# Second MLP layer by seven products of half-size blocks instead of eight, in a fused attention and MLP kernel

## The chip, the cores and the metric

The kernel runs on one core of one Trainium2 chip. The metric is device time in microseconds; the time before is the median of three runs, 341.34 us (341.12 to 341.46). Five engines work beside each other, each with its own queue in program order: TensorE (PE in the profile; its weight loads are listed apart as PEld), VectorE (DVE), ScalarE (ACT), GpSimd (POOL) and SyncE (SP), which here issues DMAs alone.

## The reference

Attention with a decay, then a two-layer MLP with gelu on its output, seen as 4608 tokens of 512 values; w_in is 512 by 2048, w_out 2048 by 512:

```python
batch, n_heads, seq, head_dim = (8, 8, 576, 64)
scores = scale * np.matmul(q, k.transpose(0, 1, 3, 2))
log_f = np.log(np.clip(f, 0.0001, 1.0))
cum = np.cumsum(log_f, axis=-1)
decay = cum[:, :, :, None] - cum[:, :, None, :]
scores = np.where(causal, -1000000000.0, scores + decay)
scores = scores - np.max(scores, axis=-1, keepdims=True)
attn = np.exp(scores)
attn = attn / (np.sum(attn, axis=-1, keepdims=True) + 1e-09)
return np.matmul(attn, v).astype(np.float32)
...
x = np.ascontiguousarray(attn_out.transpose(0, 2, 1, 3)).reshape(B * S, H * D)
...
h = x @ w_in
g = 0.5 * h * (1.0 + np.tanh(c * (h + 0.044715 * h * h * h)))
return (g @ w_out).astype(np.float32)
```

## The kernel before

**Attention** goes by quads: 16 groups of four heads of one batch, two quads to a batch. For a quad, `scores` (L202) makes the products of keys and queries in three rounds of row-tiled matmuls (32 rows, one head each) into PSUM pool `psS` (two buffers of two banks), and ScalarE takes the exponential into `pt` (L228). GpSimd masks the diagonals (`mask`, L234) and multiplies values by their decay weights (`make_vw`, L178); in FRONT some of both is on VectorE. `denominators` (word D in the tables) and `attn_out` (word V, twice a quad) are column-tiled products of 32 columns a head (L288) into pool `psO`, which has one buffer; for D, VectorE follows with a transpose, a reciprocal and a transpose (L307 to L311), for V with one multiplication into `xT` (L319). The next D or V needs psO free of these.

**The MLP** goes by chunks of 512 tokens, 0 to 8. `mlp_in` (L322) makes two blocks of 128 hidden units (a "pr") with eight matmuls of 128x512 into a psS tile; ScalarE's gelu writes them to `gT` (L337). `gT` has two buffers, by the chunk's parity. Chunk 0 goes through `mlp_in_half` (L339), in halves of 256 tokens. `mlp_out` (L357) makes the second layer: for each 128 tokens it accumulates 16 matmuls of 128x512 (stationary `gT`, moving `w_out_sb`) in a bank of pool `psM` (L91, two buffers), and VectorE copies the bank to `o_st` (L373), from where SP's queue stores it (L375).

**Order.** It is written by hand. `mlp_out` is a generator: `out_part(c, n)` (L446) pulls its next n matmuls, so that pieces of the second layer fill TensorE's time while attention waits for ScalarE. With `tiled`, which the words f of the tables and all of `beside` (L505) use, each pulled step is four column-tiled matmuls of 32 columns instead of one of 128. Setup, chunk 0, attention quads 0 to 6 and most of chunk 1 follow the word table FRONT: S and H are scores, D and V as above, M and m masks on GpSimd and VectorE, I is `mlp_in` of one pr, F and f are `out_part`, LK, LQ and LV loads, TK and TQ transposes on VectorE, X loads the table of the exponential. From chunk 2 the main loop (L550 to L564) alternates: the rest of chunk c-1's second layer, the first layer of chunk c, and in its midst `prepare` (transposes of the next quads' keys and queries on VectorE), then `pair` (L524), which runs quads 2c+3 and 2c+2 in five stages of scores, D or V and a piece of chunk c's second layer. From chunk 7 on there is no attention left: first and second layers follow each other.

Of the kernel before, what the change touches and what calls it, by code (L numbers as in the profile page):

```python
# [8 lines left out]
FP32 = mybir.dt.float32  # L9
BF16 = mybir.dt.bfloat16  # L10
AF = mybir.ActivationFunctionType
# [5 lines left out]
def kernel(  # L17
# [10 lines left out]
    nc = tc.nc  # L28

    B, H, S, D = q.shape  # L30
# [7 lines left out]
    D_MODEL, D_FF = moe_w_in.shape  # L38
    N_DT = D_MODEL // 128
    N_FT = D_FF // 128  # L40
# [4 lines left out]
    NP = D_FF // 256  # L45
    CH = 512
    NCH = B * S // CH
# [11 lines left out]
    QA = 256  # L59
# [17 lines left out]
        V.0.1.1 V.0.0.1 WO.0 J.0.1 D.1.1 J.0.0 WO.1@LV.1.1 V.1.1.1 V.1.0.1 J.0.3 WO.2@WI.1 VW.3 J.1.0 WO.3 LK.3 LQ.3 J.1.1 TQ.2 J.1.3 LQ.4  # L77
        LX.1.0@WO.2 TK.2 J.0.2 J.1.2 X LK.4 F.0.6 TK.3 B.3.256 S.2.0 LK.5 F.0.9 S.2.2 F.0.10 S.2.1 TQ.3 TQ.4 F.0.10 LV.2.0@LK.5 m.2.1 vw.2
        TK.4 S.3.0 f.0.1 M.2.2 CL.2 LQ.5 M.2.0 D.2 f.0.6 S.3.1 m.3.0 F.0.6 V.2.0 S.3.2 TK.5 LK.6 M.3.2 f.0.7 V.2.1 CL.3
        S.4.1 m.3.1 LQ.6 F.0.6 TQ.5 H.4.2.1 D.3 H.4.0.1 LQ.7 VW.4 H.4.0.0 V.3.1 v.3.0 f.0.3 H.4.2.0 CL.4 I.1.0 m.4.1 LV.2.1@LQ.5 I.1.5  # L80
        TQ.6 m.4.2.3 I.1.1 I.1.7 LV.3.0@LQ.7 m.4.2.2 TK.6 M.4.0 I.1.3 I.1.2 I.1.4 I.1.6 X F.1.8 S.5.0 F.1.2 F.1.14 S.5.1 D.4 M.5.0 f.1.9
        S.5.2 V.4.0 m.5.2.3 f.1.6 VW.5 V.4.1 CL.5 m.5.2.2 LQ.8 S.6.0 f.1.6 M.5.1 D.5 f.1.4 S.6.1 V.5.1 f.1.7 V.5.0 vw.6 S.6.2
        m.6.1 M.6.2.2 m.6.0 m.6.2.3 LK.7 LK.8 CL.6 LX.3.1@LK.6
    """

    singles = ctx.enter_context(tc.tile_pool(name="singles", bufs=1))
    ostage_pool = ctx.enter_context(tc.tile_pool(name="ostage", bufs=3))
    den_pool = ctx.enter_context(tc.tile_pool(name="den", bufs=2))
# [20 lines left out]
    gT = many(2, [128, N_FT, CH], BF16, "gT")  # L109
# [205 lines left out]
    def attn_out(i, x, spare=False, part=None):  # L315
        b, u = i // QPB, i % QPB
        po = product(i, [(32 * h, lambda t, h=h: vw[i % 2][:, t, h, x:D:2], h) for h in range(4)], spare, part)
        s0, s1 = (0, S) if part is None else parts[part]
        nc.vector.tensor_mul(xT[:, 2 * u + x, S * b + s0:S * b + s1], po, rbs[i, part])  # L319


    def mlp_in(c, prs):  # L322

        tiles = [psS.tile([128, 2, 512], FP32, name="ps_h", tag="s") for _ in prs]
        for pr, ph in zip(prs, tiles):
            for dts in (range(N_DT - 1), range(N_DT - 1, N_DT)):
                for j in range(2):
                    ft = 2 * pr + j
                    for dt in dts:
                        nc.tensor.matmul(  # L330
                            ph[:, j, :],
                            w_in_sb[:, dt, 128 * ft:128 * ft + 128],
                            xT[:, dt, CH * c:CH * (c + 1)],
                            start=(dt == 0), stop=(dt == N_DT - 1),
                        )
        for pr, ph in zip(prs, tiles):
            nc.scalar.activation(gT[c % 2][:, 2 * pr:2 * pr + 2, :], ph, AF.Gelu_apprx_tanh)  # L337

    def mlp_in_half(half, g):  # L339

        ph = psS.tile([128, 2, 512], FP32, name="ps_h", tag="s")
        n0 = QA * half
        for dts in (range(N_DT - 1), range(N_DT - 1, N_DT)):
            for j in range(4):
                ft = 4 * g + j
                for dt in dts:
                    nc.tensor.matmul(  # L347
                        ph[:, j // 2, QA * (j % 2):QA * (j % 2) + QA],
                        w_in_sb[:, dt, 128 * ft:128 * ft + 128],
                        xT[:, dt, n0:n0 + QA],  # L350
                        start=(dt == 0 and j % 2 == 0), stop=(dt == N_DT - 1),
                        skip_group_check=True,
                    )
        nc.scalar.activation(gT[0][:, 4 * g:4 * g + 4, n0:n0 + QA],
                             ph.rearrange("p a (b n) -> p (a b) n", n=QA), AF.Gelu_apprx_tanh)

    def mlp_out(c):  # L357

        for n in range(CH // 128):
            r0 = CH * c + 128 * n  # L360
            last = c == NCH - 1 and n == CH // 128 - 1
            st = ostage_pool.tile([128, D_MODEL], FP32, name="o_st", tag="o")
            for (m0, m1) in ((0, 384), (384, 512)) if last else ((0, D_MODEL),):
                pso = psM.tile([128, D_MODEL], FP32, name="pso", tag="m")
                for ft in range(N_FT):
                    cols = 32 if by_columns else 128
                    for c0 in range(0, 128, cols):
                        nc.tensor.matmul(pso[c0:c0 + cols, m0:m1],  # L368
                                         gT[c % 2][:, ft, 128 * n + c0:128 * n + c0 + cols],
                                         w_out_sb[:, ft, m0:m1],  # L370
                                         start=(ft == 0), stop=(ft == N_FT - 1), skip_group_check=True)
                    if ft == N_FT - 1:
                        nc.vector.tensor_copy(st[:, m0:m1], pso[:, m0:m1])  # L373
                        eng = nc.scalar if m0 else nc.sync
                        eng.dma_start(out=out[r0:r0 + 128, m0:m1], in_=st[:, m0:m1])  # L375
                    yield


    def setup():
# [56 lines left out]
    by_columns = []  # L436

    def pull(it, n):
        for _ in range(n):
            if next(it, False) is False:  # L440
                return

    fills = {}
    dmas = {}

    def out_part(c, n, tiled=0):  # L446
        by_columns[:] = [True] * tiled
        pull(fills.setdefault(c, mlp_out(c)), n)

    def cast_w(copy):  # L450
        copy(w_bf[:, :, 0:NT, :], wT)
# [2 lines left out]
    def load_values(b, half):  # L454
# [30 lines left out]
        "WO": load_w_out,  # L485
        "I": lambda c, pr: mlp_in(c, (pr,)),
        "J": mlp_in_half,
        "F": out_part,
        "f": lambda c, n: out_part(c, n, 1),
        "B": keep_busy,  # L490
# [3 lines left out]
    def run(table):  # L494

        for word in table.split():
            word, _, gate = word.partition("@")
            name, *args = word.split(".")
            did = ops[name](*map(int, args))
            did = did if isinstance(did, list) else [did]  # L500
            if gate:
                after(did[0], dmas[gate])
            dmas[word.replace("LP", "LU").replace("LX", "LV")] = did[-1]

    def beside(i, r, c, todo):  # L505

        if i is not None:
            scores(i, r)
        for n, x in enumerate(todo):
            if isinstance(x, int):  # L510
                out_part(c, x, 1)
# [12 lines left out]
    def pair(i, j, c):  # L524

        D, V = (lambda q: lambda: denominators(q)), (lambda q, x, spare=False: lambda: attn_out(q, x, spare))
        beside(i, 0, c, [D(j), 12])
        beside(i, 1, c, [V(j, 0), 10])
        beside(i, 2, c, [V(j, 1), 9])
        if i + 1 < NQ:  # L530
            beside(i + 1, 0, c, [D(i), 10])
            beside(i + 1, 1, c, [V(i, 0), 5, V(i, 1), 4])
            scores(i + 1, 2)
            after_scores(i + 1, 2)
        else:
            beside(None, 0, c, [D(i), 10, V(i, 0), V(i, 1, True), 10])

    def prepare(*quads):

# [56 lines left out]
```

## Time and profile before

| what | value |
|---|---|
| median of three runs | 341.34 us |
| profiled execution, span from first to last instruction | 339.9 us |
| first layer of one chunk (L330, 64 matmuls) | 13.81 us |
| second layer of chunk 7, nothing beside it (L368, 64 matmuls) | 13.81 us |
| VectorE copy of one bank to SBUF (L373, 35 times) | 687 ns each |
| ScalarE gelu of one pr (L337, 64 times) | 1024 ns each |
| DMA, mean over the span | 98 GB/s |

The page gives busy time for each engine over the span, then the same in 40 slices as tenths, with the clock that TensorE was granted. A group of instructions is one line of the program with its operation and shapes, how often it ran, its busy time and the mean of one in ns, and the idle time of its engine before it with what ended that. In a timeline a row gives the start in us, the length, the engine and the operation, neighbouring ones of a kind in one row; a matmul's length includes its way through the array, so the distance between starts tells the rate. The profile has no total for its execution besides the span.

### The profile page before, as it was taken

What the parts mean: (1) busy time and instruction counts of PE and PEld (TensorE: products, weight loads), DVE (VectorE), ACT (ScalarE), POOL (GpSimd) and SP (SyncE); (2) the same over time, 40 slices, a digit from 0 to 9 for tenths busy, and PEclk for the clock granted to TensorE, in tenths of its full rate; (3) what the DMA queues carried; (4) which work ended last, traced back from release to release, by engine and by line L of the source; (5) the groups of instructions that cost most, each with busy time, mean ns of one, the idle gap of its engine ahead of it and who ended that gap; (6) DMA issues with size and microseconds to landing.
All of it is one profiled execution on the core that took longest, in us unless ns stands there. A gap on an engine that the chain in (4) does not pass through costs nothing.

```text
span 339.9 us, 9423 instructions
## 1 busy us (share of the span) xinstructions
PE 329.8 (97%) x4241; PEld 162.0 (48%) x4241; DVE 132.3 (39%) x206; ACT 191.8 (56%) x201; POOL 110.1 (32%) x155
## 2 busy tenths in 40 slices
PE   3999999999999999999999999999999999999996
PEld 1458844544454445444444444444544454444443
DVE  4686059830465435703462244413430450021011
ACT  4784686677547665667566665674576624502510
POOL 8987551600506233601551145106410410000000
PEclk9999999999999999999999999999999999999999
DMA  7999999570316970591129210910100010011012
GB/s 127 207 216 214 196 230 194 102 172 2 95 36 101 227 156 33 131 205 39 35 77 207 59 67 35 212 30 35 63 31 2 33 63 34 2 62 62 0 40 85
DMA packets 40201, 33.26 MB, mean 98 GB/s; under 512 B 27473, under 2 KB 29777, under 8 KB 40161
## 3 DMA queue, kind: packets, MB, share of 16 engines
q0 software_dynamic: 8848, 16.58, 27.4%
q1 hardware_dynamic: 31168, 16.01, 17.0%
q8 instruction: 33, 0.54, 0.7%
q10 hardware_dynamic: 144, 0.07, 0.1%
q14 instruction: 8, 0.06, 0.0%
HBM read 36.85 MB, written 9.44 MB: 136 GB/s over the span
## 4 chain that ended last, share of the span: by engine, by line
PE 90%; DMA 2%; POOL 2%; ACT 2%; DVE 1%; issue 1%; POOLq 0%; DVEq 0%; ACTq 0%
PE pso L368 36%; PE ps_h L330 33%; PE po L288 8%; PE ps_s L220 8%; PE ps_h L347 4%; DMA v_nat<-in_v_dram 2%; ACT pt L228 2%; PE po_m L274 1%; POOL vw L178 1%; POOL v_nat L132 0%; PE ps_o L288 0%; DVE pt L263 0%; DVE vw L178 0%; POOL pt L234 0%; POOL q_c L155 0%
## 5 line engine op out<-in xcount | busy, mean ns | idle before, releaser
L368 PE MATMUL pso<-w_out_sb,gT 128*32 128x512 bf16 (+3 forms) x1492 | 134.5, 377 | 0.0
L228 ACT ACTIVATE pt<-ps_s 128x1024 bf16<-128x1024 f32 (+2 forms) x100 | 93.7, 988 | 53.6 <-PE ps_s L220 46.0
L330 PE MATMUL ps_h<-xT,w_in_sb 128*128 128x512 bf16 x512 | 111.9, 379 | 0.0
L337 ACT ACTIVATE gT<-ps_h 128x1024 bf16<-128x1024 f32 x64 | 65.5, 1024 | 64.1 <-PE ps_h L330 64.1
L234 POOL TENSOR_SCALAR_AFFINE_SELECT pt<-pt 128x512 bf16<-128x512 bf16 (+3 forms) x65 | 38.2, 597 | 140.6 <-ACT pt L228 139.7
L368 PEld LDWEIGHTS <-gT 128*32 128x32 bf16 (+1 forms) x1492 | 56.3, 97 | 56.8 <-issue 3.5
L330 PEld LDWEIGHTS <-w_in_sb 128*128 128x128 bf16 x512 | 50.0, 98 | 60.4 <-issue 0.4
L373 DVE COPY o_st<-pso 128x512 f32<-128x512 f32 (+2 forms) x37 | 24.9, 673 | 71.8 <-PE pso L368 71.5
L307 DVE STREAM_TRANSPOSE den<-po 128x576 f32<-128x576 f32 x14 | 11.0, 784 | 65.7 <-PE po L288 65.7
L220 PE MATMUL ps_s<-qT,kT 32*128 32x64 bf16 (+5 forms) x896 | 36.2, 264 | 0.2 <-ACT pt L228 0.2
L319 DVE TENSOR_TENSOR xT<-po,rb 128x576 bf16<-128x576 f32 x26 | 19.7, 757 | 31.6 <-PE po L288 31.5
L178 POOL TENSOR_TENSOR vw<-v_nat,wT 128x1280 bf16<-128x1280 f32 (+1 forms) x13 | 30.0, 2308 | 0.1
L220 PEld LDWEIGHTS <-kT 32*128 32x128 bf16 x896 | 16.4, 93 | 23.7 <-issue 18.8
L161 DVE STREAM_TRANSPOSE kT<-k_c 128x576 f32<-128x576 f32 x16 | 20.0, 1248 | 16.9 <-DMA k_c<-in_k_dram 16.8
L288 PE MATMUL po<-pt,vw 128*32 128x64 bf16 (+4 forms) x624 | 22.4, 278 | 0.0
L161 DVE STREAM_TRANSPOSE qT<-q_c 128x576 f32<-128x576 f32 x16 | 19.9, 1244 | 1.2 <-PE ps_s L220 0.7
L288 PEld LDWEIGHTS <-vw 128*32 128x32 bf16 x672 | 14.2, 97 | 11.8 <-issue 3.7
L132 POOL DMA_DIRECT2D v_nat<-in_v_dram x20 | 15.3, 776 | 3.4 <-DMA w_out_sb<-in_moe_w_out_dram 3.4
L347 PE MATMUL ps_h<-xT,w_in_sb 128*128 128x256 bf16 x128 | 14.5, 273 | 0.0
L347 PEld LDWEIGHTS <-w_in_sb 128*128 128x128 bf16 x128 | 12.3, 98 | 1.7
L311 DVE STREAM_TRANSPOSE rb<-rec 128x576 f32<-128x576 f32 (+2 forms) x18 | 12.8, 711 | 0.6
L155 POOL DMA_DIRECT2D k_c<-in_k_dram x16 | 9.1, 568 | 11.3 <-DVE kT L161 5.7
(61 smaller groups left out, 124.9 us busy)
## 6 DMA issues: line engine op xcount, KB each, us to landing
out_dram<-o_st SPq DMA_DIRECT2D x35, 256.0 KB, 2.1
k_c<-in_k_dram POOLq DMA_DIRECT2D x16, 288.0 KB, 6.8
q_c<-in_q_dram POOLq DMA_DIRECT2D x16, 288.0 KB, 7.4
v_nat<-in_v_dram SPq DMA_DIRECT2D x16, 256.0 KB, 8.3
w_in_sb<-in_moe_w_in_dram POOLq DMA_DIRECT2D x4, 512.0 KB, 9.5
w_out_sb<-in_moe_w_out_dram POOLq DMA_DIRECT2D x4, 512.0 KB, 7.2
v_nat<-in_v_dram SPq DMA_DIRECT2D x16, 128.0 KB, 3.3
v_nat<-in_v_dram POOLq DMA_DIRECT2D x13, 128.0 KB, 7.9
```

The lines of the kernel that those rows point to most:

```text
L161: nc.vector.transpose(out=dst.rearrange("p s c -> p (s c)").bitcast(FP32) .rearrange("p (t a) -> p a t", a=S // 32), in_=src.rearrange("p ...
L178: eng.tensor_mul(vw[i % 2][:, t0:t1], vb[:, t0:t1, h0:h0 + 4, :], wT[:, i, t0:t1, :].unsqueeze(3).to_broadcast([128, t1 - t0, 4, D]))
L220: nc.tensor.matmul(tiles[h // 2][:, h % 2, c0:c0 + nq], key_columns(i, key, h, c), qq[32 * h:32 * h + 32, q0:q0 + nq, c], start=(c == 0 an ...
L228: nc.scalar.activation(p[:, 2 * g:2 * g + 2, off:off + n], t[:, :, 0:n], AF.Exp, scale=scale)
L234: nc.gpsimd.affine_select(out=x, in_=x, compare_op=ALU.is_ge, fill=0.0, base=0, pattern=pattern, channel_multiplier=-1)
L288: nc.tensor.matmul(po[r0:r0 + w.shape[-1], 448 + q0:448 + q0 + nq], w, p[:, h, col:col + nq], start=(key in (0, "low")), stop=(key in ("lo ...
L319: nc.vector.tensor_mul(xT[:, 2 * u + x, S * b + s0:S * b + s1], po, rbs[i, part])
L330: nc.tensor.matmul(ph[:, j, :], w_in_sb[:, dt, 128 * ft:128 * ft + 128], xT[:, dt, CH * c:CH * (c + 1)], start=(dt == 0), stop=(dt == N_DT ...
L337: nc.scalar.activation(gT[c % 2][:, 2 * pr:2 * pr + 2, :], ph, AF.Gelu_apprx_tanh)
L347: nc.tensor.matmul(ph[:, j // 2, QA * (j % 2):QA * (j % 2) + QA], w_in_sb[:, dt, 128 * ft:128 * ft + 128], xT[:, dt, n0:n0 + QA], start=(d ...
L368: nc.tensor.matmul(pso[c0:c0 + cols, m0:m1], gT[c % 2][:, ft, 128 * n + c0:128 * n + c0 + cols], w_out_sb[:, ft, m0:m1], start=(ft == 0), ...
L373: nc.vector.tensor_copy(st[:, m0:m1], pso[:, m0:m1])
```

## The change

The second layer of chunks 1 to 8 is made by `seven_products` in place of `mlp_out`, which stays for chunk 0. The chunk of g (512 tokens by 2048) and w_out (2048 by 512) are each cut in two by two blocks: a11, a12 are the first 256 tokens with the lower and upper 1024 hidden units, a21, a22 the second 256 tokens; w11 to w22 likewise. Seven block products, each 16 matmuls of 128x256, take the place of eight. `gelu_sums` (word G) makes g1 = a21 + a22, g2 = g1 - a11, d1 = a11 - a21 (in the place of a21) and g4 = a12 - g2 on VectorE in two halves of four operations (128x1024 bf16 each); `weight_sums` (word U) makes u1 = w12 - w11, u2 = w22 - u1, u4 = w21 - u2 and w22 - w12 (in the place of w12) once, on 128x2048. The products go in turn to two PSUM banks, pa and pb; on pa each product is added to what stands there, and VectorE copies the intermediate sums (P1, V2, P7, V4) to SBUF, and adds or copies the four quarters of the result to `o_st`. `gT` has one buffer instead of two. The first layer's prs go in the order 0, 1, 4, 5, 2, 3, 6, 7. Fills that were column-tiled (f, `beside`) are full-width for these chunks, and the counts of pulled steps are new, 112 to a chunk instead of 64.

```diff
-        S.4.1 m.3.1 LQ.6 F.0.6 TQ.5 H.4.2.1 D.3 H.4.0.1 LQ.7 VW.4 H.4.0.0 V.3.1 v.3.0 f.0.3 H.4.2.0 CL.4 I.1.0 m.4.1 LV.2.1@LQ.5 I.1.5
-        TQ.6 m.4.2.3 I.1.1 I.1.7 LV.3.0@LQ.7 m.4.2.2 TK.6 M.4.0 I.1.3 I.1.2 I.1.4 I.1.6 X F.1.8 S.5.0 F.1.2 F.1.14 S.5.1 D.4 M.5.0 f.1.9
-        S.5.2 V.4.0 m.5.2.3 f.1.6 VW.5 V.4.1 CL.5 m.5.2.2 LQ.8 S.6.0 f.1.6 M.5.1 D.5 f.1.4 S.6.1 V.5.1 f.1.7 V.5.0 vw.6 S.6.2
+        S.4.1 m.3.1 LQ.6 F.0.6 TQ.5 H.4.2.1 D.3 H.4.0.1 LQ.7 VW.4 H.4.0.0 V.3.1 v.3.0 f.0.3 H.4.2.0 CL.4 I.1.0 m.4.1 U.0 LV.2.1@LQ.5 I.1.4
+        TQ.6 m.4.2.3 I.1.1 I.1.5 U.1 LV.3.0@LQ.7 m.4.2.2 TK.6 G.0 M.4.0 I.1.2 I.1.3 U.3 I.1.6 I.1.7 G.1 U.2 X F.1.14 S.5.0 F.1.28 S.5.1 D.4 M.5.0 F.1.16
+        S.5.2 V.4.0 m.5.2.3 F.1.10 VW.5 V.4.1 CL.5 m.5.2.2 LQ.8 S.6.0 F.1.10 M.5.1 D.5 F.1.7 S.6.1 V.5.1 F.1.12 V.5.0 vw.6 S.6.2
...
+    def gelu_sums(half, which=(1, 3, 2, 4)):
+        n = HF // 2
+        f0, f1 = slice(n * half, n * half + n), slice(HF + n * half, HF + n * half + n)
+        a11, a12 = gT[:, f0, 0:HC], gT[:, f1, 0:HC]
+        a21, a22 = gT[:, f0, HC:CH], gT[:, f1, HC:CH]
+        for k in which:
+            if k == 1:
+                nc.vector.tensor_add(g1[:, f0], a21, a22)
+            if k == 2:
+                nc.vector.tensor_sub(g2[:, f0], g1[:, f0], a11)
+            if k == 3:
+                nc.vector.tensor_sub(a21, a11, a21)
+            if k == 4:
+                nc.vector.tensor_sub(g4[:, f0], a12, g2[:, f0])
+
+    def seven_products(c):
...
+        def multiply(ps, x, w, first, then, ns=range(2), cols=(0, HD)):
+            for n in ns:
+                for j in range(HF):
...
+                        nc.tensor.matmul(ps[c0:c0 + width, n, cols[0]:cols[1]],
+                                         x[:, j, 128 * n + c0:128 * n + c0 + width],
+                                         w[:, j, cols[0]:cols[1]],
+                                         start=(first and n == ns[0] and j == 0), stop=(j == HF - 1),
+                                         skip_group_check=True)
+                    if n == ns[-1] and j == HF - 1:
+                        then()
+                    yield
...
+        pa, pb = bank(), bank()
+        yield from multiply(pa, a11, w11, True, lambda: keep("p1", pa))
+        yield from multiply(pb, a12, w21, True, lambda: result(0, 0, pb, kept["p1"]))
+        yield from multiply(pa, g2, u2, False, lambda: keep("v2", pa))
+        yield from multiply(pb, d1, w3, True, lambda: keep("p7", pb))
+        yield from multiply(pa, g1, u1, False, corner)
+        yield from multiply(pb, a22, u4, False, lambda: result(1, 0, pb, kept["v2"]))
+        if not last:
+            yield from multiply(pa, g4, w22, False, lambda: result(0, 1, pa))
+            return
+        for n, cols in ((0, (0, HD)), (1, (0, HD // 2)), (1, (HD // 2, HD))):
+            ps = bank()
+            yield from multiply(ps, g4, w22, True, lambda: piece(ps, n, cols), (n,), cols)
...
-        beside(i, 0, c, [D(j), 12])
-        beside(i, 1, c, [V(j, 0), 10])
-        beside(i, 2, c, [V(j, 1), 9])
+        beside(i, 0, c, [D(j), 22])
+        beside(i, 1, c, [V(j, 0), 18])
+        beside(i, 2, c, [V(j, 1), 16])
         if i + 1 < NQ:
-            beside(i + 1, 0, c, [D(i), 10])
-            beside(i + 1, 1, c, [V(i, 0), 5, V(i, 1), 4])
+            beside(i + 1, 0, c, [D(i), 18])
+            beside(i + 1, 1, c, [V(i, 0), 9, V(i, 1), 7])
...
         else:
-            beside(None, 0, c, [D(i), 10, V(i, 0), V(i, 1, True), 10])
+            beside(None, 0, c, [D(i), 18, V(i, 0), V(i, 1, True), 18])
...
             out_part(c - 1, CH)
-            for pr in range(2):
+            for pr in (0, 1):
                 mlp_in(c, (pr,))
...
-            for pr in range(2, NP):
+            for pr in (4, 5):
                 mlp_in(c, (pr,))
+            gelu_sums(0)
+            for pr in (2, 3, 6, 7):
+                mlp_in(c, (pr,))
+            gelu_sums(1)
             if c + 1 < B:
                 load_exp()
-                out_part(c, 6)
+                out_part(c, 10)
                 pair(2 * c + 3, 2 * c + 2, c)
```

`keep(name, ps)` copies a bank to a fresh SBUF tile of a pool of three; `result(i, j, x, y)` adds y to x, or copies x, into an `o_st` tile and stores it as a quarter of 256 by 256; `corner` keeps V4 and makes the result's second diagonal quarter, P7 + V4, from SBUF; `piece`, in the last chunk alone, adds V4 to a part of the last product and stores it, the very last one from ScalarE's queue.

More of the change, by code (lines that the diff above doesn't have):

```diff
@@ L87 @@
     ostage_pool = ctx.enter_context(tc.tile_pool(name="ostage", bufs=3))
+    snap_pool = ctx.enter_context(tc.tile_pool(name="snap", bufs=3))
     den_pool = ctx.enter_context(tc.tile_pool(name="den", bufs=2))
@@ L108 @@
     xT = singles.tile([128, N_DT, B * S], BF16, name="xT")
-    gT = many(2, [128, N_FT, CH], BF16, "gT")
+    HF, HD, HC = N_FT // 2, D_MODEL // 2, CH // 2
+    gT = singles.tile([128, N_FT, CH], BF16, name="gT")
+    g1, g2, g4 = many(3, [128, HF, HC], BF16, "gsum")
+    u1, u2, u4 = many(3, [128, HF, HD], BF16, "usum")
     w_in_sb = singles.tile([128, N_DT, D_FF], BF16, name="w_in_sb")
@@ L336, in mlp_in @@
         for pr, ph in zip(prs, tiles):
-            nc.scalar.activation(gT[c % 2][:, 2 * pr:2 * pr + 2, :], ph, AF.Gelu_apprx_tanh)
+            nc.scalar.activation(gT[:, 2 * pr:2 * pr + 2, :], ph, AF.Gelu_apprx_tanh)
     def mlp_in_half(half, g):
@@ L353, in mlp_in_half, with weight_sums @@
                     )
-        nc.scalar.activation(gT[0][:, 4 * g:4 * g + 4, n0:n0 + QA],
+        nc.scalar.activation(gT[:, 4 * g:4 * g + 4, n0:n0 + QA],
                              ph.rearrange("p a (b n) -> p (a b) n", n=QA), AF.Gelu_apprx_tanh)
+    def weight_sums(k):
+        w11, w12, w21, w22 = (w_out_sb[:, HF * a:HF * (a + 1), HD * b:HD * (b + 1)]
+                              for a in range(2) for b in range(2))
+        todo = ((u1, w12, w11), (u2, w22, u1), (u4, w21, u2), (w12, w22, w12))
+        nc.vector.tensor_sub(*todo[k])
@@ new lines, in seven_products, with bank, keep, result @@
+    def seven_products(c):
+        r0, last = CH * c, c == NCH - 1
+        a11, a12 = gT[:, 0:HF, 0:HC], gT[:, HF:, 0:HC]
+        d1, a22 = gT[:, 0:HF, HC:], gT[:, HF:, HC:]
+        w11, w3 = w_out_sb[:, 0:HF, 0:HD], w_out_sb[:, 0:HF, HD:]
+        w21, w22 = w_out_sb[:, HF:, 0:HD], w_out_sb[:, HF:, HD:]
+        def multiply(ps, x, w, first, then, ns=range(2), cols=(0, HD)):
+            for n in ns:
+                for j in range(HF):
+                    width = 32 if by_columns else 128
+                    for c0 in range(0, 128, width):
+                        nc.tensor.matmul(ps[c0:c0 + width, n, cols[0]:cols[1]],
[6 more added lines that the diff above has]
+                    yield
+        def bank():
+            return psM.tile([128, 2, HD], FP32, name="ps_w", tag="m")
+        kept = {}
+        def keep(name, ps):
+            kept[name] = snap_pool.tile([128, 2, HD], FP32, name="snap", tag="snap")
+            nc.vector.tensor_copy(kept[name], ps)
+        def result(i, j, x, y=None):
+            st = ostage_pool.tile([128, 2, HD], FP32, name="o_st", tag="o")
+            if y is None:
+                nc.vector.tensor_copy(st, x)
+            else:
+                nc.vector.tensor_add(st, x, y)
+            nc.sync.dma_start(
+                out=out[r0 + HC * i:r0 + HC * (i + 1), HD * j:HD * (j + 1)].rearrange("(n p) d -> p n d", p=128),
+                in_=st)
+        def corner():
+            keep("v4", pa)
+            result(1, 1, kept["p7"], kept["v4"])
+        def piece(ps, n, cols):
+            st = ostage_pool.tile([128, 2, HD], FP32, name="o_st", tag="o")
+            s = slice(*cols)
+            nc.vector.tensor_add(st[:, n, s], ps[:, n, s], kept["v4"][:, n, s])
+            eng = nc.scalar if cols[0] else nc.sync
+            eng.dma_start(out=out[r0 + 128 * n:r0 + 128 * n + 128, HD + cols[0]:HD + cols[1]], in_=st[:, n, s])
+        pa, pb = bank(), bank()
[11 more added lines that the diff above has]
+            yield from multiply(ps, g4, w22, True, lambda: piece(ps, n, cols), (n,), cols)
@@ L360, in mlp_out @@
             r0 = CH * c + 128 * n
-            last = c == NCH - 1 and n == CH // 128 - 1
             st = ostage_pool.tile([128, D_MODEL], FP32, name="o_st", tag="o")
[L363 to L376, printed above, removed]
+            pso = psM.tile([128, D_MODEL], FP32, name="pso", tag="m")
+            for ft in range(N_FT):
+                cols = 32 if by_columns else 128
+                for c0 in range(0, 128, cols):
+                    nc.tensor.matmul(pso[c0:c0 + cols, :],
+                                     gT[:, ft, 128 * n + c0:128 * n + c0 + cols],
+                                     w_out_sb[:, ft, :],
+                                     start=(ft == 0), stop=(ft == N_FT - 1), skip_group_check=True)
+                if ft == N_FT - 1:
+                    nc.vector.tensor_copy(st, pso)
+                    nc.sync.dma_start(out=out[r0:r0 + 128, :], in_=st)
+                yield
     def setup():
@@ L447, in out_part @@
         by_columns[:] = [True] * tiled
-        pull(fills.setdefault(c, mlp_out(c)), n)
+        pull(fills.setdefault(c, seven_products(c) if c else mlp_out(c)), n)
     def cast_w(copy):
@@ L487 @@
         "J": mlp_in_half,
+        "U": weight_sums,
+        "G": gelu_sums,
         "F": out_part,
@@ L510, in beside @@
             if isinstance(x, int):
-                out_part(c, x, 1)
+                out_part(c, x)
             else:
```

## The prediction

> **What bounds the kernel now.** I read the page's head and slices first, then the chain of waits, then the groups by shape, then the timeline around one attention pair.
>
> ```profile
> span 339.9 us, 9423 instructions
> PE 329.8 (97%) x4241; PEld 162.0 (48%) x4241; DVE 132.3 (39%) x206; ACT 191.8 (56%) x201; POOL 110.1 (32%) x155
> PE   3999999999999999999999999999999999999996
> DVE  4686059830465435703462244413430450021011
> PEclk9999999999999999999999999999999999999999
> ```
>
> TensorE is busy from the second slice to the last at the full granted clock. Busy time alone proves little, so the rate counts:
>
> ```profile
> 30.86 10.59 PE ps_h L347 x96
> ...
> 281.28 13.81 PE ps_h L330 x64
> 295.09 13.81 PE pso L368 x64
> ```
>
> In the chain of waits (start, length, what), 64 products of 512 columns take 13.81 us, 216 ns each, and 96 of 256 columns take 10.59 us, 110 ns each, though every one loads a new 128-column stationary operand. Both rates are nearly proportional to columns: the stream itself is the bound, from 41 us to the end. Whatever shortens it shortens the kernel, as long as nothing stops it.
>
> **Part 1, columns removed.** Chunks 1 to 8 go from 64x512 to 112x256 columns. At 109.5 ns (between the commonest distance of starts at L347, 109 ns, and the run's 110.3) a chunk costs 112 x 0.1095 = 12.26 us instead of 13.81: -1.55, times 8 = **-12.4 us**; the two ends give -12.8 and -11.7. The narrow pieces of the last chunk keep its column count.
>
> The Trainium skill (TensorE: Matmul & The Clock Gate, Back-to-back issue gap) speaks against the change: it says that in a stream of load-and-multiply pairs the spacing comes from both, 81 ns at 128 columns and 131 ns at 512. Interpolated, as an estimate, 256 columns would cost 98 ns, and 112 of those are 2.6 us more than 64 of 131, so the change would lose 21 us. Here 512 columns take 216 ns, not 131; the rows decide.
>
> **Part 2, tiling switches added.** The trace charges each switch between row-tiled scores, column-tiled attention products and full-width products:
>
> ```profile
> 83.63 3.63 PE L368 MATMUL pso<-w_out_sb,gT 128*128 128x512 bf16 x16
> 87.19 0.63 PE L220 MATMUL ps_s<-qT,kT 32*128 32x64 bf16 x16
> ```
>
> Sixteen starts at 0.2158 us lead from 83.63 to 87.08; the next kind starts 0.11 later. Single starts elsewhere give 0.09 to 0.11 for every pair of kinds (312 ns between starts where 216 is usual); I take 0.097. Before, the fill inside attention was itself column-tiled, so D or V ran into it free. Full-width, it costs one switch more in each of a pair's first four stages and three more in the fifth: 7 for each pair of chunks 2 to 5, 6 for the last pair, 7 in FRONT, 41 in all: **+4.0 us** (3.7 to 4.5).
>
> **Part 3, VectorE work, and where it stops the stream.** The prices:
>
> ```profile
> L373 DVE COPY o_st<-pso 128x512 f32<-128x512 f32 x35 | 24.1, 687 | 69.6 <-PE pso L368 69.2 <-issue 0.2
> L319 DVE TENSOR_TENSOR xT<-po,rb 128x576 bf16<-128x576 f32 x26 | 19.7, 757 | 31.6 <-PE po L288 31.5
> ...
> L263 DVE TENSOR_TENSOR pt<-pt,causal x13: 279/419/1390, 21.7 to 103.8; 128x512 bf16<-128x512 bf16 x12, 128x256 bf16<-128x256 bf16 x1
> ```
>
> The last (minimum, median and maximum) is the nearest row to a sum of halves: two bf16 operands in SBUF. 256 elements take 279 ns, 512 take 419; at 0.547 ns an element, 1024 take **0.70 us** and the 2048 of a weight sum 1.26. Upper end: 1.04 ns an element, the slope of the f32 product at L319 (757 at 576, 422 at 256), gives 1.23 us; lower end: 0.62, if the fixed part is smaller. I take 0.70, the same types and kind. Copies and additions out of PSUM cost 0.69. Successive DVE operations that don't feed each other start 0.08 before the former's end, a dependent one 0.03 after:
>
> ```profile
> 134.38 0.76 DVE L319 TENSOR_TENSOR xT<-po,rb 128x576 bf16<-128x576 f32 x1 [1.63 <-PE po L288]
> 135.06 0.68 DVE L373 COPY o_st<-pso 128x512 f32<-128x512 f32 x1
> ```
>
> DVE's own load grows by about 4.8 + 5.6 us a chunk: 39% becomes some 63%, no bound as a sum. The seven evacuations hide behind the other bank's 16 products (1.75 us against 0.2 of latency and 0.7 of copy); without that cover each costs 0.9. The weight sums U, 5.0 us, and the first four sums of g lie in the first layer's 13.8 us, where DVE idles after its transposes. The four stores have the same bytes and queue (SP) in twice the pieces; with three buffers and 2.1 us to landing they are behind nothing.
>
> What is not covered is the second G. It waits for the last gelu, and behind it in DVE's queue stands the copy of P1, without which product 3 may not write bank pa. Set the first of the remaining products at T:
>
> ```profile
> 260.73 1.46 PE L368 MATMUL pso<-w_out_sb,gT 128*128 128x512 bf16 x6
> 260.93 1.02 ACT L337 ACTIVATE gT<-ps_h 128x1024 bf16<-128x1024 f32 x1 [0.70 <-PE ps_h L330]
> 262.12 0.69 PE L220 MATMUL ps_s<-qT,kT 32*128 32x64 bf16 x24
> 262.75 0.86 PE L288 MATMUL po<-pt,w_bf 128*32 128x512 bf16 x24
> 263.44 2.76 PE L368 MATMUL pso<-w_out_sb,gT 128*32 128x512 bf16 x48
> 263.67 0.78 DVE L307 STREAM_TRANSPOSE den<-po 128x576 f32<-128x576 f32 x1 [13.61 <-PE po L288]
> ```
>
> The gelu ends at T+1.22. G runs from 1.26 for 4 x 0.70 less the overlaps = 2.68, to 3.94.
> - Chunks 7 and 8 (no attention beside): the P1 copy ends at 3.94 - 0.08 + 0.69 = 4.55; P1 and P2 end at 3.50. Stall **1.1 us** each. The last chunk adds 0.25 for its short pieces, whose banks come back later than they are refilled: 2.45 together.
> - Chunks 2 to 6: the scores wait 0.09 for the gelu's PSUM (10 products end at 1.09, before at 1.29). Between G and the copy of P1 stands D's chain (0.78 + 0.27 + 0.78), so the copy ends at about 6.4 to 6.8; product 3 arrives at 1.28 + 0.63 + 0.66 + 0.10 + 22 x 0.1093 + 0.10 + 0.57 + 0.66 + 0.10 = 6.50. Stall 0 to 0.4; I take 0.1. With 0.09: 0.2 a chunk, 1.0 together. Walking on, den, xT and the corner's two operations come before the next V by 0.2 or more, and the masks before D by 0.2.
> - Chunk 1: U.2 (1.26) also stands ahead of the copy. G from 82.43 ends at 85.1, U.2 at 86.3, the copy at 86.9; product 3 arrives at 81.18 + 1.53 + 0.10 + 0.62 + 1.97 = 85.4. Stall 1.55; DVE stays behind, and V.5.0 waits 0.35 for xT of V.5.1. **1.9 us**.
>
> Sum of stalls 2.45 + 1.0 + 1.9 = **+5.35**. With sums of 0.62 and no tail loss: 0.75 twice, 1.1, none in the pairs, 2.6 together. With sums of 1.23 (U.2 2.3): 3.2 twice and 0.25, 4.9, and five times 2.3, some 23.
>
> **The sum.** -12.4 + 4.0 + 5.35 = -3.05 on a span of 339.9, so 336.85. The profile gives no other time of that execution; the median of the runs, 341.34, is 1.44 above the span, and I carry that over: **338.3 us**.
>
> **The rivals.**
> - *DVE's chain becomes the bound.* If a sum of halves takes 1.23 us, the stalls are 23 instead of 5.35: -12.4 + 4.0 + 23 = +14.6, 356 us. It decides from about 0.79 us a sum: 34 such operations stand ahead of a copy of P1 (four in each of eight chunks, and U.2 counts double), so 0.09 more on each eats the 3.05. For it: one of the thirteen bf16 products took 1390 ns, with POOL issuing loads at the time. Against: the median 419, and POOL's masks start after G (265.35 against T + 3.94 = 264.67). The Trainium skill (SBUF — State Buffer, Who interferes with whom) says that a DVE instruction with two SBUF inputs and a GpSimd one that reads SBUF lock each other out; no row here separates that.
> - *Small waits eat the gain:* psO (one buffer, freed by DVE's den or xT) coming back 0.2 us later than my walk at three of the five stages of five pairs is 3.0, at all five with 0.3 it is 7.5: 341 to 345. For it: slack of only 0.1 to 0.2 us at V(i,0) to V(i,1) (xT ends 0.09 before the next V now). Against: every fill is of two-bank turns, not one.
> - *The stalls vanish* because DVE overlaps better: -12.4 + 4.0 + 2.6 = -5.8, and with switches at 0.09 and products at 109 ns -6.5: 334.8 to 335.5. For it: DVE idles 61% now. Against: it needs the one price that I could not read off an equal row to lie at its lower end.
> - *The products are no faster*, the load of the stationary operand showing at 256 columns. L347 has the same shape and load and does not show it; 3%.
>
> **How the numbers follow.** Forecast (336 to 340.6) 0.46; stalls vanish 0.14; small waits 0.22, of which a third within noise; DVE chain 0.15; slow products 0.03. A measurement of this kernel tells 0.2% (0.7 us) from no change: faster 0.60, same 0.10, slower 0.30. The range takes in the vanished stalls and the small waits, and a tenth above for the chain: 334.2 to 345; the forecast's own is 336 to 340.6.
>
> **What would show it.** Second-layer products 109 ns apart; 41 more switches; G operations at 0.70; a PE gap ahead of product 3 of about 1.1 us in chunks 7 and 8, 1.5 in chunk 1, next to none in chunks 2 to 6, each ended by DVE. G at 1.2 us, or gaps ended by den or xT in the pairs, would make the forecast wrong.

## The result and the profile after

| | median | lowest to highest | runs |
|---|---|---|---|
| before | 341.43 us | 340.95 to 345.14 | 11 |
| after | 344.92 us | 344.53 to 345.63 | 11 |

The ratio is 1.0086, with a 95% interval from 1.0058 to 1.0114: 0.9% slower, where 0.9% faster was forecast. The profiled execution of after has a span of 343.0 us against 339.9, so it shows the whole difference. (Executions more than 1.5% above the fastest of their kernel are left out of the ratios and of the medians of e5 and e10; the only trace of e10 is of such a one, at a mean clock of 0.855, so no times are read from it.) From the page of after:

```profile
span 343.0 us, 8601 instructions
PE 322.6 (94%) x3748; PEld 196.5 (57%) x3768; DVE 199.3 (58%) x307; ACT 191.2 (56%) x201; POOL 110.6 (32%) x155
PE   3999999999899999999999999999999999989984
```

TensorE is busy 7.2 us less than before (329.8), but the span is 3.1 us longer: the products did become cheaper, and some 10 us of standing still came in. The groups by shape (line, engine, operation, output from input, count, busy time and mean ns of one, idle time before) show that the new work costs what was forecast:

```profile
L397 PE MATMUL ps_w<-usum,gsum 128*128 128x256 bf16 x256 | 32.0, 273 | 3.5 <-DVE snap L413 3.5
...
L413 DVE COPY snap<-ps_w 128x512 f32<-128x512 f32 x32 | 21.6, 676 | 12.9 <-PE ps_w L397 12.9
...
L376 DVE TENSOR_TENSOR gsum<-gT 128x1024 bf16<-128x1024 bf16 x16 | 11.1, 692 | 66.3 <-ACT gT L341 66.3
L420 DVE TENSOR_TENSOR o_st<-ps_w,snap 128x512 f32<-128x512 f32 x16 | 11.0, 688 | 1.8 <-PE ps_w L397 1.1
```

A sum of halves takes 0.68 to 0.69 us (0.70 was put in), a copy or addition out of PSUM 0.68 to 0.69. The 273 ns of a product include its way through the array; the median distance between the starts of successive ones is 109 ns. What TensorE waited for stands in the waits (engine, line, what for: us in total, times, longest):

```profile
PE ps_h L334 <- ACT gT L341: 4.3, 6, 0.7
...
PE ps_w L397 <- DVE snap L413: 3.5, 3, 1.4
...
DVE o_st L432 <- DMA out_dram<-o_st: 0.8, 1, 0.8
...
PE po L292 <- DVE xT L323: 0.3, 1, 0.3
```

The second and fourth rows are the forecast's stalls, ahead of product 3 (chunks 1, 7, 8) and at V.5.0. The first and third are not in the forecast. The first sits in the first layer, which the change touched only by the order of its prs. Here is the start of chunk 2's first layer before the change, in the timeline:

```profile
103.27 13.98 PE L330 MATMUL ps_h<-xT,w_in_sb 128*128 128x512 bf16 x64
103.64 1.28 ACT L337 ACT_TABLE_LOAD   x1
...
105.19 1.02 ACT L337 ACTIVATE gT<-ps_h 128x1024 bf16<-128x1024 f32 x1 [0.27 <-PE ps_h L330]
```

And after it:

```profile
104.19 3.62 PE L334 MATMUL ps_h<-xT,w_in_sb 128*128 128x512 bf16 x15
...
106.15 1.28 ACT L341 ACT_TABLE_LOAD   x1 [1.52 <-issue]
...
107.45 1.94 ACT L341 ACTIVATE gT<-ps_h 128x1024 bf16<-128x1024 f32 x2
108.52 3.83 PE L334 MATMUL ps_h<-xT,w_in_sb 128*128 128x512 bf16 x17 [0.71 <-ACT gT L341]
```

Before, ScalarE changes its table from the exponential to gelu while TensorE makes the first pr, 0.37 us after its start; the gelu is ready when the products are. After, the load starts 1.96 us after the first product, when that pr is complete. Both of psS's buffers are then full, and the third pr waits: its first product would start 16 x 0.2158 = 3.45 us after 104.19, at 107.64, and starts at 108.52. That is **0.88 us, in each of chunks 2 to 7, 5.3 together**. The trace for the gelu's own line says what has changed on ScalarE's queue, before:

```profile
L337 ACTq EVENT_SEMAPHORE  x8: 17/17/17, 310.7 to 322.8; - x8
```

and after:

```profile
L341 ACTq EVENT_SEMAPHORE  x56: 17/17/14812, 102.8 to 325.0; - x56
```

These are wait instructions of their own (minimum, median and maximum ns, first and last start): eight before, 56 after. Of the first one the same view, from 100 to 107 us, says:

```profile
L341 ACTq EVENT_SEMAPHORE  x1: 3374/3374/3374, 102.8 to 102.8; - x1
```

It stands ahead of the table load and lasts 3.37 us, until the products of the first pr are complete (106.12); the load starts 0.03 us later. The end shows the other new wait:

```profile
336.48 2.16 PE L397 MATMUL ps_w<-w_out_sb,gsum 128*128 128x256 bf16 x24
...
338.00 1.37 SPq L434 DMA_DIRECT2D out_dram<-o_st  x2
...
339.77 0.29 DVE L432 TENSOR_TENSOR o_st<-ps_w,snap 128x128 f32<-128x128 f32 x1 [0.77 <-DMA out_dram<-o_st]
```

The products end at 336.48 + 2.16 = 338.64, and the addition before ends at 339.0; the very last addition still waits 0.77 us for one of the three `o_st` tiles, from which a store is under way.

**The account.** Forecast for the span 336.85, plus 5.28 for the six gaps and 0.77 for the tail: 342.9; the span is 343.0. Setup, ahead of all this, took 0.2 us less in this trace than in the one of before; counted from the first layer of chunk 1 on, the change costs 3.3 us where the account has 3.0.

### The profile page after: what moved, and what is told of

It reads as the page before. It is cut to its first block, busy times and chain, and to the rows that moved or that the text cites. A ratio compares the mean times of both kernels' runs of the same rounds, so it can differ in the third digit from the quotient of the medians.

```text
span 343.0 us, 8601 instructions
## 1 busy us (share of the span) xinstructions
PE 322.6 (94%) x3748; PEld 196.5 (57%) x3768; DVE 199.3 (58%) x307; ACT 191.2 (56%) x201; POOL 110.6 (32%) x155
## 5 line engine op out<-in xcount | busy, mean ns | idle before, releaser
L341 ACT ACTIVATE gT<-ps_h 128x1024 bf16<-128x1024 f32 x64 | 64.9, 1024 | 51.4 <-PE ps_h L334 45.5
L334 PEld LDWEIGHTS <-w_in_sb 128*128 128x128 bf16 x512 | 49.9, 98 | 64.3 <-issue 6.4
L397 PEld LDWEIGHTS <-gT 128*128 128x128 bf16 x512 | 48.3, 98 | 9.5 <-issue 0.2
L376 DVE TENSOR_TENSOR gsum<-gT 128x1024 bf16<-128x1024 bf16 x16 | 11.1, 692 | 66.3 <-ACT gT L341 66.3
L397 PE MATMUL ps_w<-w_out_sb,gT 128*128 128x256 bf16 x384 | 46.6, 273 | 0.0
L397 PEld LDWEIGHTS <-gsum 128*128 128x128 bf16 x392 | 36.3, 98 | 10.8 <-issue 5.4
L224 PE MATMUL ps_s<-qT,kT 32*128 32x64 bf16 (+5 forms) x896 | 36.9, 264 | 0.3 <-ACT pt L232 0.2
L397 PE MATMUL ps_w<-usum,gsum 128*128 128x256 bf16 x256 | 32.0, 273 | 3.5 <-DVE snap L413 3.5
L413 DVE COPY snap<-ps_w 128x512 f32<-128x512 f32 x32 | 21.6, 676 | 12.9 <-PE ps_w L397 12.9
L341 ACT ACT_TABLE_LOAD x7 | 9.0, 1283 | 16.3 <-issue 16.3
L397 PE MATMUL ps_w<-usum,gT 128*128 128x256 bf16 x128 | 17.0, 273 | 0.0
```

What stands on the lines that cost most here:

```text
L224: nc.tensor.matmul(tiles[h // 2][:, h % 2, c0:c0 + nq], key_columns(i, key, h, c), qq[32 * h:32 * h + 32, q0:q0 + nq, c], start=(c == 0 an ...
L334: nc.tensor.matmul(ph[:, j, :], w_in_sb[:, dt, 128 * ft:128 * ft + 128], xT[:, dt, CH * c:CH * (c + 1)], start=(dt == 0), stop=(dt == N_DT ...
L341: nc.scalar.activation(gT[:, 2 * pr:2 * pr + 2, :], ph, AF.Gelu_apprx_tanh)
L397: nc.tensor.matmul(ps[c0:c0 + width, n, cols[0]:cols[1]], x[:, j, 128 * n + c0:128 * n + c0 + width], w[:, j, cols[0]:cols[1]], start=(fir ...
L413: nc.vector.tensor_copy(kept[name], ps)
```

## The experiments

Two explanations of the six gaps were open. *Theory A:* the gelu has one more thing to wait for, since gT now has one buffer; a wait of its own then stands in ScalarE's queue, and the table load, which belongs to the gelu, comes after it. *Rival B:* the load is incidental, and the single buffer itself makes the first layer late. Times below are medians; a ratio is to the kernel before, run on the same chip.

**e1: the table is loaded ahead of the gelu,** by a gelu of one element that waits for no other engine.

```diff
+    def load_gelu():
+        nc.scalar.activation(spare, shift[0:1, :], AF.Gelu_apprx_tanh)
...
         for c in range(2, NCH):
+            if c < B:
+                load_gelu()
             out_part(c - 1, CH)
```

> The changed kernel, and ahead of the second layer's remainder in chunks 2 to 7 a 1x1 gelu on ScalarE, so that the gelu table is loaded before the first gelu's wait. Theory A (the wait on VectorE for the one gT buffer became an instruction of its own in front of the table load, so that the load of 1.28 us now starts only when the first pr's products are done): the six PE gaps of 0.88 us at the start of the first layer go, 344.9 - 5.3 = 339.6 us. Rival B (the gelu is held because the single gT buffer is still being read, wherever the table load stands): the gaps stay and the time stays at 344.9. Rival C (the surplus lies in the stalls behind the copy of P1): less than 1 us better.

339.32 us (338.84 to 340.88), ratio 0.9933 [0.9915, 0.9952]: 5.6 less than after. The timeline of e1 at the place shown above:

```profile
104.03 8.15 PE L338 MATMUL ps_h<-xT,w_in_sb 128*128 128x512 bf16 x37
104.49 1.28 ACT L200 ACT_TABLE_LOAD   x1
...
105.79 0.20 ACT L200 ACTIVATE spare<-shift 1x1 f32<-1x1 f32 x1
...
105.96 1.02 ACT L345 ACTIVATE gT<-ps_h 128x1024 bf16<-128x1024 f32 x1
```

The load follows the exponential at once, and TensorE runs through. All six gaps are gone and the stalls ahead of product 3 stand as they were. gT still has its one buffer and 32 separate waits of the gelu are left: where the load stands is what cost the time. The Trainium skill (ScalarE: Activation LUTs, What ACT_TABLE_LOAD costs) gives 1283 ns for the load, as here, and some 1380 ns for a drain; these rows show none, since the load starts 0.02 us after the exponential's end and the next activation 0.02 us after the load's.

**e5: the kernel before, with one gT buffer and nothing else of the change.**

```diff
-    gT = many(2, [128, N_FT, CH], BF16, "gT")
+    gT = many(1, [128, N_FT, CH], BF16, "gT")
...
-            nc.scalar.activation(gT[c % 2][:, 2 * pr:2 * pr + 2, :], ph, AF.Gelu_apprx_tanh)
+            nc.scalar.activation(gT[0][:, 2 * pr:2 * pr + 2, :], ph, AF.Gelu_apprx_tanh)
```

> The kernel before with one gT buffer in place of two and nothing else. Theory A: no VectorE operation reads gT here, the first gelu waits for PE alone, which its own products make it do anyway; no wait stands in front of the table load, and the time stays at 341.4 within 0.3. Rival B (one gT buffer holds the gelu by itself): six gaps of about 0.9, 346.7 us.

346.52 us (346.38 to 347.30, three runs), ratio 1.0144 [1.0113, 1.0175]. As it was put, theory A falls: it asked for a second engine (VectorE's sums) to be waited for, and there is none here. The timeline of e5:

```profile
103.63 3.62 PE L330 MATMUL ps_h<-xT,w_in_sb 128*128 128x512 bf16 x16
...
105.60 1.28 ACT L337 ACT_TABLE_LOAD   x1 [1.62 <-PE ps_h L330]
...
106.90 1.94 ACT L337 ACTIVATE gT<-ps_h 128x1024 bf16<-128x1024 f32 x2
107.97 3.40 PE L330 MATMUL ps_h<-xT,w_in_sb 128*128 128x512 bf16 x15 [0.72 <-ACT gT L337]
```

The same picture, late load and all: the next product starts 4.34 us after the first, 0.89 late, as after. The first gelu of the chunk waits for the products by an instruction of its own, ahead of the load, and then itself for the earlier write of the same buffer by its own engine. So a second wait of whatever kind suffices (theory A2), or else it is B.

**e6: e5 with e1's early load.**

> The kernel before with one gT buffer, and the 1x1 gelu ahead of the second layer's remainder in chunks 2 to 7. Theory A as it was put has fallen: with one buffer the kernel before lost 5.3 us without any VectorE work on gT. Theory A2: any second wait will do (here the gelu waits for its own engine's earlier write of the same buffer), since the wait for PE then becomes an instruction of its own in front of the table load; with the load made early the six gaps of 0.89 us go, 341.6 us. Rival B (the one buffer holds the gelu back wherever the load stands): 346.9 us.

341.50 us (340.97 to 341.85), ratio 0.9983 [0.9954, 1.0012]: with one gT buffer the kernel is as fast as with two. Rival B falls. One thing e6 leaves open by itself: with the early load, e5's 53 separate waits are eight again, so load and waits left together. In e1, 32 stayed, and the gaps still went; but those of chunks 2 to 7, 24 of them, are for VectorE and not for the products. That a wait for the products costs nothing by itself shows in after: ahead of later gelus of chunk 2 there is such a wait without a load behind it (one of 1.65 us from 112.26), and these gelus start 1.73 us apart, the time of their eight products.

**e2: the sums that product 3 doesn't need go behind the copy of P1.** Product 3 reads g2 alone; d1 and g4 were made ahead of it.

```diff
-            gelu_sums(1)
+            gelu_sums(1, (1, 2))
...
-        yield from multiply(pa, a11, w11, True, lambda: keep("p1", pa))
+        yield from multiply(pa, a11, w11, True, lambda: (keep("p1", pa), gelu_sums(1, (3, 4))))
...
-G.1 U.2 X F.1.14 S.5.0 F.1.28 S.5.1
+G.1.1.2 X F.1.14 S.5.0 F.1.28 U.2 S.5.1
```

> The changed kernel with another order on VectorE alone: of the second G only g1 and g2 stay ahead of the copy of P1, d1 and g4 follow it, and U.2 stands behind the copy too. The stalls ahead of product 3 (1.57 us in chunk 1, 1.22 each in chunks 7 and 8) and V.5.0's wait of 0.39 should go, at most 0.1 left: 344.9 - 4.3 = 340.6 us by theory A, with the six gaps of 0.88 still there. Rival C (all the surplus of the result over the forecast, 6.6 us, comes from VectorE's queue): 338 us or less. If the copy is held by something else than the sums ahead of it: 344.9.

340.82 us (340.22 to 341.40), ratio 0.9976 [0.9964, 0.9988]. Of TensorE's waits in after, the row of three stalls ahead of product 3 (3.5 us) is gone; these two stay:

```profile
PE ps_h L334 <- ACT gT L341: 4.3, 6, 0.7
...
PE po L292 <- DVE xT L323: 0.3, 1, 0.3
```

344.92 - 340.82 = 4.1, against 1.57 + 2 x 1.22 = 4.0 measured in after. That part of the forecast was right in kind and size. V.5.0's wait, which was expected to go with it, stayed.

**e3: the fill inside attention column-tiled again,** in `beside` and in FRONT.

```diff
-                out_part(c, x)
+                out_part(c, x, 1)
```

> The changed kernel with the fill inside attention column-tiled again, as before the change (four products of 32 columns a step). By the price of a switch, 0.097 us, 41 fewer give 344.9 - 4.0 = 340.9 us, if four column-tiled products of 256 columns take the 109 ns of one full one. Rival D (four times the instructions at 256 columns can't be issued in 109 ns; half as long as the 216 ns that they had before): each of some 90 steps in a pair takes up to 60 ns more and eats the gain: 344.9 or slower, up to 30 us.

342.52 us, ratio 1.002 [1.0, 1.004]: -2.4 instead of -4.0. From chunk 3 on a chunk with its pair gets shorter by 0.59, near the 7 x 0.097 put in; but there are two waits more, 0.7 us together, which nothing in the profile releases, and V.5.0 waits longer for xT (0.5 by the waits instead of 0.3). Column-tiling has a price of its own, then, to which e9 returns.

**e7: the last chunk's two narrow pieces share an `o_st` tile.**

```diff
-            st = ostage_pool.tile([128, 2, HD], FP32, name="o_st", tag="o")
+            if not cols[0]:
+                kept["st"] = ostage_pool.tile([128, 2, HD], FP32, name="o_st", tag="o")
+            st = kept["st"]
```

> The changed kernel, the last chunk's two narrow pieces in one o_st tile in place of two. Theory: the very last addition waits 0.77 us for the store of the quarter three tiles earlier; with one tile fewer it doesn't: 344.9 - 0.8 = 344.1 us. Rival: the wait is in the shadow of the store that comes after it, or the store's own length sets the end: 344.9.

344.04 us, ratio 1.0063 [1.0029, 1.0096], 0.88 less than after: the wait for the store was on the path for its whole 0.77.

**e8: e1, e2 and e7 together.**

> The changed kernel with the early table load, the other VectorE order and the shared o_st tile together, fills full-width. If the parts are independent: 344.9 - 5.6 - 4.1 - 0.8 = 334.4 us. If one hides behind another (the gaps give VectorE time to catch up): up to 1.5 more.

334.88 us (334.02 to 337.96, 4 runs), ratio 0.98 [0.974, 0.986]. The single gains, 5.6, 4.1 and 0.9, add up to 10.6; 344.92 - 334.88 = 10.0. This is the forecast's change without its large stalls: -12.4 + 4.0, with the small ones left (0.39 at V.5.0, 1.0 in chunks 2 to 6, 0.25 at the end), make -6.8; to the kernel before beside it (341.49) it is -6.6.

**e9: e8 with e3's column-tiled fill.**

> As the run before, with the fill inside attention column-tiled. By the price of a switch (41 x 0.097) 4.0 us less, 330.4; by what tiling alone gave (2.4, with new stalls of VectorE in chunks 1 and 2) 332.0. Rival D (the issue of small products costs): 334.4 or more.

333.03 us, ratio 0.9739 [0.9693, 0.9786]. Chunks 4 and 5 take 34.46 us each against 35.16 in e8, 0.70 for seven switches, 0.10 a switch. But chunk 2 takes 36.05 against 35.17. The timeline of e9, TensorE alone:

```profile
123.09 1.26 PE L401 MATMUL ps_w<-usum,gsum 128*32 128x256 bf16 x39
125.67 0.92 PE L401 MATMUL ps_w<-usum,gsum 128*32 128x256 bf16 x25 [1.31 <-issue]
```

In the middle of one run of products TensorE stops for 1.31 us, and no semaphore ends it: "issue" is waiting for nothing that the profile shows. A column-tiled step is four instructions instead of one. The instruction DMA of e9 moves 41 packets, that of e8 29; one of them starts at 122.68 and takes 1.47 us, so it ends at 124.15, 1.52 us before the products go on. *Theory E:* TensorE has run out of instructions because that fetch is late behind the loads of attention's inputs, which are heavy here. *Rival F:* the higher rate alone suffices, wherever the first tiled stretch stands.

Chunk 3 of e9 takes 34.80, 0.33 more than the next two, and there too TensorE stops between two products of one run. The same 56 products take 1.70 us in one place and 2.04 in another:

```profile
162.46 1.70 PE L401 MATMUL ps_w<-w_out_sb,gT 128*32 128x256 bf16 x56
...
165.63 2.04 PE L401 MATMUL ps_w<-usum,gsum 128*32 128x256 bf16 x56
```

From 165.85 to the next start 0.33 us pass, where 0.03 are usual, and nothing releases it.

**e10: tiled fill in the pairs from chunk 3 on** (on e8; also one step moved from the first stage to ahead of it, here and in e11).

```diff
-                out_part(c, x)
+                out_part(c, x, c > 2)
```

> The full-width combination (early table load, other VectorE order, shared o_st tile; 334.9 us), with the fill column-tiled in the pairs of chunks 3 to 6 alone, and one product more ahead of a pair's first scores (11 and 21 for 10 and 22). Theory E: the 1.3 us for which PE waited for nothing in the pair of chunk 2, where an instruction fetch of the profile was under way and the loads held 60% of the DMA engines, is the fetch of four times the instructions, late behind the loads; from chunk 3 on the engines are mostly free, so no such gap: -0.70 each in three pairs, -0.43 in the last, -0.1 for each pair's first scores: 331.8 us. Rival F (the gap comes from the number of instructions, wherever it starts): a gap of about 1.3 us turns up in chunk 3's pair, 333.1 us.

332.55 us (331.78 to 332.84, five runs), ratio 0.9724 [0.9695, 0.9752], between the two. Its trace can't decide about the gap.

**e11: tiled fill in the fifth stage of each pair only,** where it saves three switches at once; and FRONT's piece beside V.5.0.

```diff
-            beside(i + 1, 1, c, [V(i, 0), 9, V(i, 1), 7])
+            beside(i + 1, 1, c, [V(i, 0), 9, V(i, 1), 7], 1)
```

> The same combination with the fill column-tiled only between the two V of a pair's fifth stage (and of V.5.1 and V.5.0), where full-width costs three switches, and the 11 and 21 products. Theory by the price of a switch: 4 pairs x 3 x 0.097 + 0.2 + 0.5 = 1.9 us less than 334.9: 333.0 us. If the gain of tiling comes from all stages only together, 334.4.

333.08 us (332.78 to 334.50), ratio 0.9741 [0.9713, 0.9769]: the price of a switch once more, and no gap. FRONT's piece gave nothing: chunk 1 takes 35.53 us against 35.54 in e8, since V.5.0 waits 0.4 for xT instead of 0.3.

**e12: e10 and e11 together,** with a trace that can answer the question of e9.

> The fill of chunks 3 to 5 column-tiled in every stage of the pairs (as in e10), that of chunk 2 only in the fifth stage (as in e11), and FRONT's last piece column-tiled too. Theory E (the unreleased gap of e9 needs the loads of chunk 2 beside it): no TensorE gap over 0.3 us inside the pairs of chunks 3 to 5, their periods 34.5 us as in e9's chunks 4 and 5, that of chunk 2 34.85 as in e11; time 332.65 (e10) - 3 x 0.097 (fifth stage of chunk 2) - 2 x 0.097 (FRONT's piece) = 332.2. Rival F (the first tiled stretch of the pairs stalls, wherever it is): a gap of 1 us or more at the first tiled fill of chunk 2 or in chunk 3's first stages, time 333 or more.

**331.15 us** (330.85 to 331.31, 4 runs), ratio 0.9689 [0.9673, 0.9705]: 3.1% faster than before, the best version. Windows of 13 us from the first stages of a pair, of e9 (chunk 2, tiled):

```profile
117.00:130.00 13.00, 11.69 (x370) 8.85 (x371) 8.58 (x14) 8.14 (x9) 4.59 (x5) 1.00 0.60 124
```

and of e12 (chunk 2 not tiled, chunk 3 tiled); the second number is TensorE's busy time with its instructions, the last but one the mean busy share of the DMA engines:

```profile
115.00:128.00 13.00, 13.00 (x201) 8.99 (x200) 8.95 (x14) 9.17 (x10) 4.29 (x5) 1.00 0.74 152
150.00:163.00 13.00, 13.00 (x375) 9.55 (x377) 8.65 (x14) 9.00 (x10) 4.63 (x6) 1.00 0.21 53
```

370 matmuls beside a DMA share of 0.60 lose 1.31 us; 201 beside 0.74 lose nothing, and neither do 375 beside 0.21. Rival F falls as it was put: the first pair that is tiled throughout, now that of chunk 3, runs without a stop. But theory E is not shown either, for shorter stops came while the DMA engines stood idle. This is e9 around the stop of 165.85:

```profile
164.00:167.00 3.00, 2.95 (x105) 1.89 (x97) 1.76 (x4) 1.89 (x2) 1.17 (x2) 1.00 0.00 0
```

One of the two stops of e3 is of this kind too: 0.55 us between two starts at 94.76, with a DMA share of 0.00 from 94.0 to 95.4. What the four stops of e3 and e9 have in common is that the products go on 1.4 to 1.6 us after an instruction packet has landed. That speaks for the fetch, but most packets are followed by no stop, and no run delayed a fetch by itself: what stops TensorE here stays open. Chunks 3 and 4 take 34.39 us each, chunk 2 34.83, as expected. The time is 1.05 below the expected 332.2, and that is not explained, since e10, from which the figure started, has no usable trace.

Setup, which no part of the change touches, moves by up to 2.0 us from execution to execution: the first layer of chunk 1 starts at 66.79 in the trace of e3, at 67.13 in that of e12 and at 68.76 in that of e11. Single spans should be compared from there on.

## Why the prediction was wrong

Point by point, by its own steps:

- **Part 1, columns removed, -12.4: right.** Products start 109 ns apart. The rule of the Trainium skill that was weighed against the rows (TensorE: Matmul & The Clock Gate, Back-to-back issue gap) would, by the prediction's estimate, have made the change lose 21 us; the rows were right.
- **Part 2, switches, +4.0: right.** In after, 205 ns lie between the starts at a switch from products to scores where 109 are usual; undoing seven switches gave 0.59 (e3) and 0.70 (e9).
- **Part 3, stalls of VectorE, +5.35: right in place and nearly in size.** Ahead of product 3: 1.57 in chunk 1 (1.55 forecast), 1.22 in chunks 7 and 8 (1.1). V.5.0: 0.39 over the usual switch (0.35). The short last pieces: their 24 products take 2.16 us where 8 x 0.109 + 16 x 0.055 + 0.16 for the way through the array make 1.91 (0.25 forecast). In chunks 2 to 6 nothing beyond the forecast's 0.2: without the 0.88, a chunk takes 35.22 us against 35.24 by the forecast's terms.
- **What VectorE does in all: put too high.** Some 63% of the span was forecast, 58% measured (199.3 us): the 4.8 us a chunk are seven evacuations of 0.69, and the four copies that they replace were not taken off. Nothing else of the sum hangs on it.
- **From the span to the time:** 1.44 us were carried over; in after it is 1.7 (344.71 against 343.0 in the profiled execution), 0.3 of the miss.
- **What failed: "gT has one buffer instead of two" was described in the change and given no term in the sum.** It is a step like the others, and its cost of 5.3 us is larger than the whole gain forecast (3.05). The question that the prediction asked of every other edit, who waits for it and what is behind the waiting instruction, was asked of VectorE's queue and SP's, not of ScalarE's. The traces show what stands there: a table load, cheap for as long as it can start under the first pr's products, and 0.88 us on the path of TensorE as soon as a wait for those products stands in front of it. "The scores wait 0.09 for the gelu's PSUM" looked at the right pool, at its other user.
- **"The stores ... are behind nothing" failed at the end of the kernel:** there five stores follow within 4 us of each other, and the last addition waits 0.77 us for one.
- **The rivals.** VectorE's chain did not become the bound (0.69 us a sum, the break at 0.79). On the interference with GpSimd the prediction said that no row separates it; one does, in the trace before: at 103.84 a product of L263 (median 419 ns) takes 853 ns while GpSimd has a mask from 103.69 to 104.42. "Small waits" forecast 341 to 345 and the time fell there, but by another mechanism: its psO waits sum to 0.3 us. That the time lies just inside the upper end of the range, 345.0, is owed to no step of it.

## What to carry to other kernels

When a change takes a buffer away or adds a reader to it, list the instructions that now need one more wait, and see what their engine does on their behalf just ahead of them: a table load behind a wait can't be hidden. A table switch wants an instruction of its own, at the first idle moment, waiting for no other engine (here a gelu of one element: 5.6 us for one line). Between a product and the copy that frees its bank, put only what that copy or the next product needs; the remaining sums can run behind it (here 4.1 us for the other order).

## What the runs showed of the hardware

- **A separate wait ahead of an activation moves its table load too:** the load, 1283 ns, starts 1.96 us after the first product instead of 0.37, with no change to the activation itself (after; the same in e5), and an early load takes it off the path (e1, e6).
- **TensorE can stop within a run of column-tiled products with nothing in the profile that releases it:** 1.31 us at 370 matmuls in 13 us with the DMA engines 0.60 busy and 0.3 us with them idle (e9); not at 201 and 0.74 or 375 and 0.21 (e12). The cause is open.
- **VectorE beside GpSimd:** in each of the five pairs of e9 the sum d1 takes longer than its equals (as in e2, e8, e11 and e12, 1.05 to 1.08 us):

```profile
121.96 1.08 DVE L384 TENSOR_TENSOR gT<-gT 128x1024 bf16<-128x1024 bf16 x1
122.96 0.68 DVE L386 TENSOR_TENSOR gsum<-gT,gsum 128x1024 bf16<-128x1024 bf16 x1
```

  1.08 us against 0.69, while GpSimd works on a mask (121.36 to 122.49). The Trainium skill (SBUF — State Buffer, Who interferes with whom) has the two engines share a pair of ports under a lock; the row agrees with it. In after the sums ended before the masks began, as the prediction had it, and none took longer.
